# Residual adds as identity matmuls into PSUM, and second-LayerNorm sums from ScalarE, in an attention + GEGLU block

## The chip, the cores and the metric

One core of one Trainium2 chip runs the whole block in one launch. The metric is device time in microseconds (us). Before the change the median of the first four runs was 1486.33 us (1484.91 to 1489.46). The profile is one execution; its span is about 1.7 us shorter than the timed run.

Engine names in profile lines: PE is TensorE (matmul), PEld its weight load, DVE is VectorE, ACT is ScalarE, POOL is GpSimd.

## The reference

2048 tokens of width 512, 32 heads of width 16, FFN width 1792, all bf16:

```python
h  = x + attention(layernorm(x)) @ wo
h2 = h + (gelu(layernorm(h) @ w_gate) * (layernorm(h) @ w_up)) @ w_down
```

Two residual adds and a second LayerNorm (LN2) lie between the matmuls. They are what the change moves.

## The kernel before

The kernel is one list of "ticks", 1024 of them for the row maxima (phase 1) and 1024 for the exps (phase 2), 42 ticks apart. In each tick TensorE makes two score tiles that VectorE max-reduces and, of an earlier unit, two transposed score tiles that ScalarE exponentiates into bf16. A *unit* is 32 ticks: four heads against 512 queries. Eight units make a *chunk* of 512 tokens. Three PSUM banks serve phase 1 and three serve phase 2, and all four matmuls of a tick wait together:

```python
P.group_begin("pe")
t1  = p1_pair(tick // 32, tick % 32, gp1, signal_last=not p2_ok) if p1_ok else []
t2l = p2_pair(t2 // 32, t2 % 32, 1 - gp1) if p2_ok else []
P.group_end("pe")            # moves all waits of the four matmuls to the first
...                          # p1_consume: two max-reduces on VectorE
...                          # p2_consume: two exps on ScalarE
```

Everything else (Q/K/V projections, output projection, FFN) is cut into pieces of two or three matmuls, and one piece goes into each tick. When a piece is done, its PSUM bank has to be emptied; most items do so with an "evacuation" on ScalarE. Two kinds of item used VectorE instead. `item_oproj` (attention output projection, four per chunk) and `item_down` (FFN down projection, four per chunk):

```python
def item_oproj(b, c, qt):
    ...                                     # four matmuls into pbank[:, b, :]
    dve_late_ns[0] += 1480                  # asks for filler matmuls, see below
    P.op("dve", tensor_tensor(out=hh[:, qt, :], in0=pbank[:, b, :], in1=xres[:, xi, :], op=add))
    P.op("dve", bn_stats(out=stats2[:, t, :], in_=hh[:, qt, :]))
    P.op("dve", bn_aggr(out=mv2[:, t, :], in_=stats2[:, t, :]))
    ...                                     # POOL: rstd, -mean*rstd, normalise into hn_sb

def item_down(b, c, qt):
    ...                                     # fourteen matmuls into pbank[:, b, :]
    dve_late_ns[0] += 690
    P.op("dve", tensor_tensor(out=out_sb[:, oi, :], in0=pbank[:, b, :], in1=hh[:, qt, :], op=add))
    ...                                     # DMA to the output
```

(The lines are shortened: argument lists of the planner are left out.) After a tick with such VectorE work the loop adds filler matmuls, one for each 230 ns of it:

```python
if dve_late_ns[0] and p2_started and p1_ok:
    dummy(3 + p2_ring[0] % 3, dve_late_ns[0] // 230)
```

The fourth chunk's second half comes after all ticks; there is no attention to share time with any more. This is called the *tail*.

## Time and profile before

| what | before |
|---|---|
| median time | 1486.33 us (first four runs), 1489.15 (13 runs) |
| span of the profile | 1487.7 us |
| end of the last phase-1 unit | 1373.7 us |
| busy VectorE / ScalarE / TensorE | 89% / 86% / 77% |

The busy totals are the first part of the page:

```profile
PE 1142.3 (77%) x8558; PEld 310.6 (21%) x8558; DVE 1322.2 (89%) x2206; ACT 1274.8 (86%) x2414; POOL 453.1 (30%) x557
```

The groups of instructions (line, engine, operation, shapes, count; then busy time and mean ns of one; then idle time before them and what ended it):

```profile
L554 DVE TENSOR_REDUCE PM<-pbank 128x1 f32<-128x512 f32 x2048 | 1255.9, 683 | 62.3 <-PE pbank L595 49.3 <-PE pbank L545 12.0
L605 ACT ACTIVATE PT<-pbank 128x512 bf16<-128x512 f32 x2048 | 1116.6, 601 | 107.8 <-PE pbank L595 36.8
...
L695 DVE BATCH_NORM_STATS2 stats<-h_c 128x6 f32<-128x512 bf16 x16 | 11.1, 694 | 0.6
L794 DVE TENSOR_TENSOR out_sb<-pbank,h_c 128x512 bf16<-128x512 f32 x16 | 11.0, 686 | 56.9 <-PE pbank L787 56.9
L693 DVE TENSOR_TENSOR h_c<-pbank,xres 128x512 bf16<-128x512 f32 x16 | 10.9, 684 | 11.1 <-PE pbank L687 11.1
```

The first two groups are the attention itself. Busy time over count gives 0.613 us per max-reduce and 0.545 us per exp, so a tick of two of each needs 1.23 us on VectorE and 1.09 us on ScalarE. The mean duration (683 and 601 ns) is longer, because consecutive instructions of an engine overlap.

The timeline of VectorE around one oproj item shows the interruption. Columns: start, duration, engine, line, operation, shapes, count.

```profile
446.07 2.48 DVE L554 TENSOR_REDUCE PM<-pbank 128x1 f32<-128x512 f32 x4 [0.17 <-PE pbank L595]
448.47 0.68 DVE L693 TENSOR_TENSOR h_c<-pbank,xres 128x512 bf16<-128x512 f32 x1
449.19 0.69 DVE L695 BATCH_NORM_STATS2 stats<-h_c 128x6 f32<-128x512 bf16 x1
449.92 0.18 DVE L696 BATCH_NORM_AGGREGATE mv<-stats 128x2 f32<-128x6 f32 x1
450.01 2.45 DVE L554 TENSOR_REDUCE PM<-pbank 128x1 f32<-128x512 f32 x4
452.50 0.26 DVE L559 TENSOR_REDUCE NEGM<-PM 128x16 f32<-128x64 f32 x1
```

From 448.47 to 450.01 us the max-reduces stand still: 1.54 us. The last line (128x16) is the end of a unit. It comes once in 32 ticks, so the distance between two of these is the length of a unit, and that repeats to a few hundredths of a us. Here are the engines' busy times in five units, which differ in what else they hold: three ScalarE extras and nothing more; one oproj; three oproj; FFN (12 ScalarE extras); two down items.

```profile
core 0: us, PE busy (x) PEld busy (x) DVE busy (x) ACT busy (x) POOL busy (x), PEclk, DMA share, GB/s
372.02:411.37 39.35, 31.50 (x247) 7.48 (x246) 38.81 (x66) 35.88 (x68) 4.53 (x6) 1.00 0.01 1
411.37:452.50 41.13, 32.55 (x260) 8.41 (x258) 40.35 (x69) 36.27 (x69) 6.48 (x11) 1.00 0.05 14
452.50:497.21 44.71, 34.21 (x278) 9.96 (x275) 43.45 (x75) 37.67 (x72) 10.67 (x22) 1.00 0.00 1
538.37:579.87 41.50, 30.88 (x250) 7.75 (x246) 39.56 (x66) 39.42 (x77) 22.62 (x24) 1.00 0.00 1
704.34:745.00 40.66, 34.23 (x265) 8.96 (x262) 40.12 (x67) 36.07 (x69) 7.62 (x9) 1.00 0.02 8
```

The first unit is the attention alone, 39.35 us. One oproj makes it 41.13, three make it 44.71, two down items 40.66 (0.65 us per add). In the row with three oproj VectorE is busy 43.45 of 44.71 us and ScalarE only 37.67: VectorE sets these units. In the FFN row both are busy about 39.5 of 41.5.

In the tail the VectorE adds follow the matmuls at a steady distance:

```profile
1437.28 0.69 DVE L693 TENSOR_TENSOR h_c<-pbank,xres 128x512 bf16<-128x512 f32 x1 [1.37 <-PE pbank L687]
...
1440.28 0.69 DVE L693 TENSOR_TENSOR h_c<-pbank,xres 128x512 bf16<-128x512 f32 x1 [1.36 <-PE pbank L687]
...
1481.78 0.69 DVE L794 TENSOR_TENSOR out_sb<-pbank,h_c 128x512 bf16<-128x512 f32 x1 [2.33 <-PE pbank L787]
1484.81 0.69 DVE L794 TENSOR_TENSOR out_sb<-pbank,h_c 128x512 bf16<-128x512 f32 x1 [2.33 <-PE pbank L787]
```

That is 3.00 us between oproj items, 3.03 between down items; TensorE's matmuls make up most of it.

### The profile page before, as it was taken

What the parts mean: (1) busy time and instruction counts of PE and PEld (TensorE: products, weight loads), DVE (VectorE), ACT (ScalarE), POOL (GpSimd) and SP (SyncE); (2) the same over time, 40 slices, a digit from 0 to 9 for tenths busy, and PEclk for the clock granted to TensorE, in tenths of its full rate; (3) what the DMA queues carried; (4) which work ended last, traced back from release to release, by engine and by line L of the source; (5) the groups of instructions that cost most, each with busy time, mean ns of one, the idle gap of its engine ahead of it and who ended that gap; (6) DMA issues with size and microseconds to landing.
All of it is one profiled execution on the core that took longest, in us unless ns stands there. A gap on an engine that the chain in (4) does not pass through costs nothing.

```text
span 1487.7 us, 24868 instructions
## 1 busy us (share of the span) xinstructions
PE 1142.3 (77%) x8558; PEld 310.6 (21%) x8558; DVE 1322.2 (89%) x2206; ACT 1274.8 (86%) x2414; POOL 453.1 (30%) x557
## 2 busy tenths in 40 slices
PE   4977777777777777777887777777887777777879
PEld 2311111111112211111222211111222211111224
DVE  5989999998999999999999999999999999998023
ACT  3469999997998999999888999999888999999942
POOL 6001011110112255554112255554112255554130
PEclk9999999999999999999999999999999999999969
DMA  3000000012000000000000000000000000000000
GB/s 113 1 1 2 1 2 2 2 73 77 1 16 1 2 1 1 1 1 2 8 23 1 2 1 1 1 1 1 9 23 2 1 2 1 1 1 2 8 22 15
DMA packets 11531, 15.88 MB, mean 11 GB/s; under 512 B 1040, under 2 KB 9872, under 8 KB 11408
## 3 DMA queue, kind: packets, MB, share of 16 engines
q1 hardware_dynamic: 11408, 14.29, 2.8%
q8 instruction: 71, 1.16, 0.3%
q14 instruction: 52, 0.43, 0.1%
HBM read 11.80 MB, written 2.10 MB: 9 GB/s over the span
## 4 chain that ended last, share of the span: by engine, by line
DVE 37%; ACT 27%; PE 18%; issue 16%; POOL 1%; DMA 1%; SPq 0%; POOLq 0%; ACTq 0%
DVE PM L554 34%; ACT PT L605 23%; PE pbank L545 11%; PE pbank L787 2%; PE pbank L595 1%; PE pbank L480 1%; PE pbank L744 1%; PE pbank L763 1%; ACT OA L443 1%; ACT u_sb L443 1%; DVE stats L311 1%; DVE stats L695 1%; ACT g_sb L443 1%; DVE h_c L693 1%; PE pbank L687 1%
## 5 line engine op out<-in xcount | busy, mean ns | idle before, releaser
L554 DVE TENSOR_REDUCE PM<-pbank 128x1 f32<-128x512 f32 x2048 | 1255.9, 683 | 62.3 <-PE pbank L595 49.3
L605 ACT ACTIVATE PT<-pbank 128x512 bf16<-128x512 f32 x2048 | 1116.6, 601 | 107.8 <-PE pbank L595 36.8
L545 PE MATMUL pbank<-KT,QT 32*128 32x512 bf16 x2048 | 398.7, 384 | 301.4 <-DVE PM L554 169.2
L595 PE MATMUL pbank<-QT,KT 32*128 32x512 bf16 x2048 | 397.9, 385 | 3.2 <-ACT PT L605 2.7
L801 PE MATMUL pbank<-ones_bf,ident 128*128 128x512 bf16 x910 | 282.9, 384 | 1.3
L545 PEld LDWEIGHTS pbank<-KT,QT 32*128 32x128 bf16 x2048 | 103.8, 91 | 773.6 <-DVE PM L554 760.6
L639 POOL TENSOR_TENSOR LINV<-OAT,negone 128x16 f32<-128x16 f32 x32 | 93.3, 2916 | 351.6 <-ACT OAT L443 351.6
L616 PE MATMUL pbank<-PT,VA 128*17 128x512 bf16 x2048 | 156.7, 383 | 0.0
L565 POOL CAST ST<-NEGM 128x16 bf16<-128x16 f32 x32 | 8.1, 254 | 320.3 <-DVE NEGM L559 320.3
L595 PEld LDWEIGHTS pbank<-QT,KT 32*128 32x128 bf16 x2048 | 96.1, 91 | 22.4 <-ACT PT L605 21.9
L801 PEld LDWEIGHTS pbank<-ones_bf,ident 128*128 128x128 bf16 x910 | 61.7, 97 | 120.8 <-ACT PT L605 91.6
L722 POOL TENSOR_TENSOR w_sb<-g_sb 128x512 f32<-128x512 f32 x42 | 43.7, 1041 | 136.0 <-ACT g_sb L443 136.0
L744 PE MATMUL pbank<-hnT_c,wg_sb 128*128 128x512 bf16 x224 | 67.0, 392 | 0.9 <-ACT hnT_c L443 0.7
L763 PE MATMUL pbank<-hnT_c,wu_sb 128*128 128x512 bf16 x224 | 66.3, 388 | 0.0
L794 DVE TENSOR_TENSOR out_sb<-pbank,h_c 128x512 bf16<-128x512 f32 x16 | 11.0, 686 | 56.9 <-PE pbank L787 56.9
L787 PE MATMUL pbank<-wd_sb,GUT 128*128 128x512 bf16 x224 | 58.6, 382 | 2.2
L776 POOL TENSOR_TENSOR GUT<-th_sb,u_sb 128x512 bf16<-128x512 f32 x42 | 53.2, 1266 | 14.5 <-ACT u_sb L443 13.3
L724 POOL TENSOR_TENSOR w_sb<-w_sb,g_sb 128x512 f32<-128x512 f32 x42 | 53.3, 1269 | 3.5
L728 POOL TENSOR_TENSOR th_sb<-th_sb,g_sb 128x512 f32<-128x512 f32 x42 | 53.2, 1267 | 3.5
L616 PEld LDWEIGHTS pbank<-PT,VA 128*17 128x17 bf16 x2048 | 28.3, 87 | 58.7 <-issue 58.4
L441 ACT ACTIVATE KT<-pbank,kbias 128x512 bf16<-128x512 f32 x32 | 22.1, 689 | 19.2 <-PE pbank L480 19.2
L480 PE MATMUL pbank<-xnT,wk_pad 128*128 128x512 bf16 x128 | 37.8, 412 | 0.8
(75 smaller groups left out, 667.5 us busy)
## 6 DMA issues: line engine op xcount, KB each, us to landing
x_sb<-in_A_x_dram SPq DMA_DIRECT2D x4, 512.0 KB, 5.5
QT<-STG SPq DMA_DIRECT2D x128, 3.0 KB
xres<-in_A_x_dram SPq DMA_DIRECT2D x16, 128.0 KB, 2.2
out_dram<-out_sb SPq DMA_DIRECT2D x16, 128.0 KB, 1.7
wg_sb<-in_B_w_gate_dram SPq DMA_DIRECT2D x1, 1792.0 KB, 7.1
wu_sb<-in_B_w_up_dram SPq DMA_DIRECT2D x1, 1792.0 KB, 11.1
wd_sb<-in_B_w_down_dram SPq DMA_DIRECT2D x1, 1792.0 KB, 17.1
wqkv_sb<-in_A_wqkv_dram SPq DMA_DIRECT2D x1, 1536.0 KB, 10.3
```

The source lines that it names most:

```text
L545: P.op("pe", lambda e, g=g, b=b: e.matmul(pbank[:, b, :], QT[32 * g:32 * g + 32, c, slot, 128 * qt:128 * qt + 128], KT[32 * g:32 * g + 32, ...
L554: P.op("dve", lambda e, b=b, qt=qt, kc=kc, g=g: e.tensor_reduce(out=PM[:, par, qt, kc, g:g + 1], in_=pbank[:, b, :], axis=AX.X, op=ALU.max ...
L595: P.op("pe", lambda e, g=g, b=b: e.matmul(pbank[:, b, :], KT[32 * g:32 * g + 32, slot, 128 * kt:128 * kt + 128], QT[32 * g:32 * g + 32, c, ...
L605: P.op("act", lambda e, b=b, pi=pi: e.activation(out=PT[:, pi, :], in_=pbank[:, b, :], func=ACT.Exp), reads=[("pb", b)], writes=[("PT", pi)])
L616: P.op("pe", lambda e, g=g, kt=kt, pi=pi, slot=slot: e.matmul(pbank[32 * g:32 * g + 17, PVB, :], VA[:, kt, 4 * slot + g, :], PT[:, pi, :], ...
L639: P.op("pool", lambda e: e.tensor_tensor(out=li, in0=oat4[:, :, :, 16], in1=negone[:].rearrange("p (q g) -> p q g", g=4), op=ALU.pow), rea ...
L724: P.op(eng, lambda e: e.tensor_tensor(out=ws, in0=ws, in1=gs, op=ALU.mult), reads=[("w", par), ("g", par)], writes=[("w", par)])
L728: P.op(eng, lambda e: e.tensor_tensor(out=ts_, in0=ts_, in1=gs, op=ALU.mult), reads=[("th", par), ("g", par)], writes=[("th", par)])
L744: P.op("pe", lambda e, dc=dc: e.matmul(pbank[:, b, :], wg_sb[:, dc, 128 * fc:128 * fc + 128], hT[:, dc, :], start=(dc == 0), stop=(dc == 3 ...
L763: P.op("pe", lambda e, dc=dc: e.matmul(pbank[:, b, :], wu_sb[:, dc, 128 * fc:128 * fc + 128], hT[:, dc, :], start=(dc == 0), stop=(dc == 3 ...
L787: P.op("pe", lambda e, fc=fc: e.matmul(pbank[:, b, :], GUT[:, fc, 128 * qt:128 * qt + 128], wd_sb[:, fc, :], start=(fc == 0), stop=(fc == ...
L801: P.op("pe", lambda e: e.matmul(pbank[:, b, :], ident[:], ones_bf[:, 0:512], start=True, stop=True), reads=["ident", "ones_bf"], writes=[( ...
```

## The change

The intent is to relieve VectorE. The residual is added by TensorE: a matmul of the identity with the residual tile accumulates it into the same PSUM bank. ScalarE then copies the finished sum out, and its accumulator output gives the row sum of h. A second ScalarE pass (Square with accumulation) gives the sum of squares, and POOL makes mean and variance from the two sums. The tail keeps VectorE, with a copy in place of the add. The filler requests of these two items are dropped.

```diff
 def item_oproj(b, c, qt):
-    four matmuls, the last with stop=True
-    dve_late_ns[0] += 1480
-    dve: h = pbank + xres ; bn_stats(h) ; bn_aggr
-    return 2
+    four matmuls, none with stop
+    P.op("pe", matmul(pbank[:, b, :], ident[:], xres[:, xi, :], start=False, stop=True))
+    if tail_mode[0]:
+        dve: h = copy(pbank) ; bn_stats(h) ; bn_aggr ; ln2_tail ; return 3
+    P.op("act", activation(out=hh[:, qt, :], in_=pbank[:, b, :], func=Copy, accum_out=hsum[:, t:t+1]))
+    def sq():                     # put off while this or the last tick has a ScalarE extra
+        P.op("act", activation(out=sqj[:], in_=hh[:, qt, :], func=Square, accum_out=hsq[:, t:t+1]))
+        defer(1, lambda: ln2_from_sums(c, qt, t))     # POOL: mean, E[h^2] - mean^2, rstd, normalise
+    defer(2, sq)
+    return 3
 ...
 def item_down(b, c, qt):
-    fourteen matmuls, the last with stop=True
-    dve_late_ns[0] += 690
-    dve: out_sb = pbank + h
+    fourteen matmuls, none with stop
+    P.op("pe", matmul(pbank[:, b, :], ident[:], hh[:, qt, :], start=False, stop=True))
+    dve (tail): out_sb = copy(pbank)    else act: out_sb = Copy(pbank)
```

(Abbreviated; helpers and clean-ups without effect are left out.)

More of the change, by code (lines that the diff above doesn't have):

```diff
@@ L278, in bass_sequential_preLN__mha_block__geglu_ffn__prompt_kernel @@
         nmr1 = at("nmr1", [128, NT], FP32)
+        hsum = at("hsum", [128, NT], FP32)
+        hsq = at("hsq", [128, NT], FP32)
+        htmp = at("htmp", [128, NT], FP32)
+        sqj = at("sqj", [128, 512], BF16)
         pbank = es.enter_context(nc.psum_tensor("pbank", [128, 8, 512], FP32))
@@ L413, in defer @@
             deferred.append((dense.now + k, fn))
+        force = [False]
         def run_deferred(now, flush=False):
+            if flush:
+                force[0] = True
             i = 0
@@ L420, in run_deferred, with evac_act @@
                     i += 1
-        def halves(ap):
-            n = ap.shape[-1]
-            h = n // 2
-            idx0 = tuple([slice(None)] * (len(ap.shape) - 1) + [slice(0, h)])
-            idx1 = tuple([slice(None)] * (len(ap.shape) - 1) + [slice(h, n)])
-            return ap[idx0], ap[idx1]
         act_extra = set()
-        def evac_act(o_ap, i_ap, reads, writes, scale=None, extra=(), bias=None, split=False, then=None):
+        def evac_act(o_ap, i_ap, reads, writes, scale=None, extra=(), bias=None, then=None):
             act_extra.add(dense.now)
-            def one(o, i):
-                kw = {}
-                if scale is not None:
-                    kw["scale"] = scale
-                if bias is not None:
-                    P.op("act", lambda e: e.activation(out=o, in_=i, func=ACT.Identity, bias=bias, **kw), reads=list(reads) + ["kbias"], writes=writes, extra_deps=extra)
-                else:
-                    P.op("act", lambda e: e.activation(out=o, in_=i, func=ACT.Copy, **kw), reads=reads, writes=writes, extra_deps=extra)
-            if not split or not dense.single:
-                one(o_ap, i_ap)
-                if then is not None:
-                    then()
-                return
-            o0, o1 = halves(o_ap)
-            i0, i1 = halves(i_ap)
-            one(o0, i0)
-            for w in writes:
-                P.held.add(w)
-            def second():
-                for w in writes:
-                    P.held.discard(w)
-                one(o1, i1)
-                if then is not None:
-                    then()
-            defer(1, second)
+            kw = {}
+            if scale is not None:
+                kw["scale"] = scale
+            if bias is not None:
+                P.op("act", lambda e: e.activation(out=o_ap, in_=i_ap, func=ACT.Identity, bias=bias, **kw), reads=list(reads) + ["kbias"], writes=writes, extra_deps=extra)
+            else:
+                P.op("act", lambda e: e.activation(out=o_ap, in_=i_ap, func=ACT.Copy, **kw), reads=reads, writes=writes, extra_deps=extra)
+            if then is not None:
+                then()
         region = {}
@@ L498, in item_projV @@
                     yield 2
-            pv3 = pbank[:, b, :].rearrange("p (h i) -> p h i", i=16)
-            if False:
-                P.op("act", lambda e: e.activation(out=VA[:, t, 0:16, 0:16], in_=pv3[:, 0:16, :], func=ACT.Copy), reads=[("pb", b)], writes=[("V", t)])
-                P.held.add(("V", t))
-                def vsecond():
-                    P.held.discard(("V", t))
-                    P.op("act", lambda e: e.activation(out=VA[:, t, 16:32, 0:16], in_=pv3[:, 16:32, :], func=ACT.Copy), reads=[("pb", b)], writes=[("V", t)])
-                defer(1, vsecond)
-            else:
-                P.op("act", lambda e: e.activation(out=VA[:, t, :, 0:16], in_=pv3, func=ACT.Copy), reads=[("pb", b)], writes=[("V", t)])
+            evac_act(VA[:, t, :, 0:16], pbank[:, b, :].rearrange("p (h i) -> p h i", i=16), [("pb", b)], [("V", t)])
             qkv_left[0] -= 1
@@ L646, in item_ofin @@
             return 1
+        out_n = [0]
         chunk_units_done = {}
@@ L685, in item_oproj @@
             xi = qt
+            hh = h_c[c]
             for hc in range(4):
-                P.op("pe", lambda e, hc=hc: e.matmul(pbank[:, b, :], OnT[:, qt, hc, :], wo_sb[:, hc, :], start=(hc == 0), stop=(hc == 3)),
-                     reads=[("OH", qt), "wo"], writes=[("pb", b)], sig=(hc == 3))
+                P.op("pe", lambda e, hc=hc: e.matmul(pbank[:, b, :], OnT[:, qt, hc, :], wo_sb[:, hc, :], start=(hc == 0), stop=False),
+                     reads=[("OH", qt), "wo"], writes=[("pb", b)], sig=False)
@@ L689, in item_oproj @@
                 if hc == 1:
                     yield 2
-            hh = h_c[c]
-            dve_late_ns[0] += 1480
-            P.op("dve", lambda e: e.tensor_tensor(out=hh[:, qt, :], in0=pbank[:, b, :], in1=xres[:, xi, :], op=ALU.add),
-                 reads=[("pb", b), ("xres", xi)], writes=[("h", c, qt)], extra_deps=dQ)
-            P.op("dve", lambda e: e.bn_stats(out=stats2[:, t, :], in_=hh[:, qt, :]), reads=[("h", c, qt)], writes=[("stats2", t)])
-            P.op("dve", lambda e: e.bn_aggr(out=mv2[:, t, :], in_=stats2[:, t, :]), reads=[("stats2", t)], writes=[("mv2", t)])
@@ L697, in item_oproj @@
-            P.op("pool", lambda e: e.tensor_scalar(out=rstd2[:, t:t + 1], in0=mv2[:, t, 1:2], scalar1=EPS, scalar2=None, op0=ALU.add), reads=[("mv2", t)], writes=[("rstd2", t)])
-            P.op("pool", lambda e: e.tensor_tensor(out=rstd2[:, t:t + 1], in0=rstd2[:, t:t + 1], in1=nhalf[:, 0:1], op=ALU.pow), reads=[("rstd2", t), "nhalf"], writes=[("rstd2", t)])
-            P.op("pool", lambda e: e.tensor_tensor(out=nmr2[:, t:t + 1], in0=mv2[:, t, 0:1], in1=rstd2[:, t:t + 1], op=ALU.mult), reads=[("mv2", t), ("rstd2", t)], writes=[("nmr2", t)])
@@ L700, in item_oproj @@
-            P.op("pool", lambda e: e.tensor_scalar(out=nmr2[:, t:t + 1], in0=nmr2[:, t:t + 1], scalar1=-1.0, scalar2=None, op0=ALU.mult), reads=[("nmr2", t)], writes=[("nmr2", t)])
-            P.op("pool", lambda e: e.tensor_scalar(out=hn_sb[:, qt, :], in0=hh[:, qt, :], scalar1=rstd2[:, t:t + 1], scalar2=nmr2[:, t:t + 1], op0=ALU.mult, op1=ALU.add),
+            P.op("pe", lambda e: e.matmul(pbank[:, b, :], ident[:], xres[:, xi, :], start=False, stop=True),
+                 reads=["ident", ("xres", xi)], writes=[("pb", b)], sig=True)
@@ new lines, in item_oproj @@
+            if tail_mode[0]:
+                P.op("dve", lambda e: e.tensor_copy(out=hh[:, qt, :], in_=pbank[:, b, :]), reads=[("pb", b)], writes=[("h", c, qt)], extra_deps=dQ)
+                P.op("dve", lambda e: e.bn_stats(out=stats2[:, t, :], in_=hh[:, qt, :]), reads=[("h", c, qt)], writes=[("stats2", t)])
+                P.op("dve", lambda e: e.bn_aggr(out=mv2[:, t, :], in_=stats2[:, t, :]), reads=[("stats2", t)], writes=[("mv2", t)])
+                ln2_tail(c, qt, t)
+                return 3
@@ new lines, in item_oproj @@
+            act_extra.add(dense.now)
+            P.op("act", lambda e: e.activation(out=hh[:, qt, :], in_=pbank[:, b, :], func=ACT.Copy, accum_out=hsum[:, t:t + 1]),
+                 reads=[("pb", b)], writes=[("h", c, qt), ("hsum", t)], extra_deps=dQ)
+            def sq():
+                if not force[0] and ((dense.now in act_extra) or ((dense.now - 1) in act_extra and dense.now - 1 != sq_t0[0])):
+                    defer(1, sq)
+                    return
+                act_extra.add(dense.now)
+                P.op("act", lambda e: e.activation(out=sqj[:], in_=hh[:, qt, :], func=ACT.Square, accum_out=hsq[:, t:t + 1]),
+                     reads=[("h", c, qt)], writes=[("sqjunk",), ("hsq", t)])
+                defer(1, lambda: ln2_from_sums(c, qt, t))
@@ new lines, in item_oproj, with ln2_from_sums @@
+            sq_t0 = [dense.now]
+            defer(2, sq)
+            return 3
+        def ln2_from_sums(c, qt, t):
+            hh = h_c[c]
+            tt_ = slice(t, t + 1)
+            P.op("pool", lambda e: e.tensor_scalar(out=mv2[:, t, 0:1], in0=hsum[:, tt_], scalar1=1.0 / D, scalar2=None, op0=ALU.mult), reads=[("hsum", t)], writes=[("mv2", t)])
+            P.op("pool", lambda e: e.tensor_tensor(out=htmp[:, tt_], in0=mv2[:, t, 0:1], in1=mv2[:, t, 0:1], op=ALU.mult), reads=[("mv2", t)], writes=[("htmp", t)])
+            P.op("pool", lambda e: e.tensor_scalar(out=rstd2[:, tt_], in0=hsq[:, tt_], scalar1=1.0 / D, scalar2=EPS, op0=ALU.mult, op1=ALU.add), reads=[("hsq", t)], writes=[("rstd2", t)])
+            P.op("pool", lambda e: e.tensor_tensor(out=rstd2[:, tt_], in0=rstd2[:, tt_], in1=htmp[:, tt_], op=ALU.subtract), reads=[("rstd2", t), ("htmp", t)], writes=[("rstd2", t)])
+            ln2_finish(c, qt, t)
@@ new lines, in ln2_tail, with ln2_finish @@
+        def ln2_tail(c, qt, t):
+            tt_ = slice(t, t + 1)
+            P.op("pool", lambda e: e.tensor_scalar(out=rstd2[:, tt_], in0=mv2[:, t, 1:2], scalar1=EPS, scalar2=None, op0=ALU.add), reads=[("mv2", t)], writes=[("rstd2", t)])
+            ln2_finish(c, qt, t)
+        def ln2_finish(c, qt, t):
+            hh = h_c[c]
+            tt_ = slice(t, t + 1)
+            P.op("pool", lambda e: e.tensor_tensor(out=rstd2[:, tt_], in0=rstd2[:, tt_], in1=nhalf[:, 0:1], op=ALU.pow), reads=[("rstd2", t), "nhalf"], writes=[("rstd2", t)])
+            P.op("pool", lambda e: e.tensor_tensor(out=nmr2[:, tt_], in0=mv2[:, t, 0:1], in1=rstd2[:, tt_], op=ALU.mult), reads=[("mv2", t), ("rstd2", t)], writes=[("nmr2", t)])
+            P.op("pool", lambda e: e.tensor_scalar(out=nmr2[:, tt_], in0=nmr2[:, tt_], scalar1=-1.0, scalar2=None, op0=ALU.mult), reads=[("nmr2", t)], writes=[("nmr2", t)])
+            P.op("pool", lambda e: e.tensor_scalar(out=hn_sb[:, qt, :], in0=hh[:, qt, :], scalar1=rstd2[:, tt_], scalar2=nmr2[:, tt_], op0=ALU.mult, op1=ALU.add),
@@ L729, in later @@
             def later():
-                if dense.single and (dense.now in act_extra or (dense.now - 1) in act_extra):
+                if not force[0] and (dense.now in act_extra or (dense.now - 1) in act_extra):
                     defer(1, later)
@@ L778, in item_up @@
             return 2
-        out_n = [0]
         def item_down(b, c, qt):
@@ L785, in item_down @@
                 yield ("wait", 7)
+            hh = h_c[c]
             for fc in range(NFC):
-                P.op("pe", lambda e, fc=fc: e.matmul(pbank[:, b, :], GUT[:, fc, 128 * qt:128 * qt + 128], wd_sb[:, fc, :], start=(fc == 0), stop=(fc == NFC - 1)),
-                     reads=[("GUT", fc), "wd"], writes=[("pb", b)], sig=(fc == NFC - 1))
+                P.op("pe", lambda e, fc=fc: e.matmul(pbank[:, b, :], GUT[:, fc, 128 * qt:128 * qt + 128], wd_sb[:, fc, :], start=(fc == 0), stop=False),
+                     reads=[("GUT", fc), "wd"], writes=[("pb", b)], sig=False)
                 if fc % 3 == 2:
                     yield 3
+            P.op("pe", lambda e: e.matmul(pbank[:, b, :], ident[:], hh[:, qt, :], start=False, stop=True),
+                 reads=["ident", ("h", c, qt)], writes=[("pb", b)], sig=True)
             oi = out_n[0] % 2; out_n[0] += 1
-            hh = h_c[c]
-            dve_late_ns[0] += 690
-            P.op("dve", lambda e: e.tensor_tensor(out=out_sb[:, oi, :], in0=pbank[:, b, :], in1=hh[:, qt, :], op=ALU.add),
-                 reads=[("pb", b), ("h", c, qt)], writes=[("osb", oi)], extra_deps=dG)
+            if tail_mode[0]:
+                P.op("dve", lambda e: e.tensor_copy(out=out_sb[:, oi, :], in_=pbank[:, b, :]), reads=[("pb", b)], writes=[("osb", oi)], extra_deps=dG)
+            else:
+                evac_act(out_sb[:, oi, :], pbank[:, b, :], [("pb", b)], [("osb", oi)], extra=dG)
             P.dma("sp", lambda e: e.dma_start(out=outv[:, t, :], in_=out_sb[:, oi, :]), ("out", oi), reads=[("osb", oi)], writes=[("outd", t)])
-            return 2
+            return 3
         def dummy(b, n):
```

## The prediction

> **What bounds the kernel now.** Span 1487.7 us; the page's busy table gives VectorE 89%, ScalarE 86%, TensorE 77%. The main part (1024 ticks, to 1374 us) issues per tick two score tiles that VectorE max-reduces and two that ScalarE exponentiates; a tick lasts as long as the slower. Busy time over count: a max-reduce occupies VectorE 0.613 us (1255.9/2048), an exp ScalarE 0.545 (1116.6/2048): 1.23 against 1.09 us per tick.
>
> The timeline shows one row-max finish (128x16 reduce) per unit of 32 ticks; unit lengths price the extras:
> - 3 ScalarE extras, no VectorE extra: 39.35 us. An isolated evacuation costs one 0.17 us VectorE gap.
> - 12 ScalarE extras (FFN): 41.5, so about 0.23 us each of their 0.6.
> - one oproj item: add 0.68, stats 0.69, aggregate 0.18, in all 1.54 us. Unit with one: 41.13; with three: 44.71.
> - two down adds: 40.66, +0.65 each.
>
> After 1374 us VectorE idles and ScalarE runs exps back to back (39 in 21.68 us): every extra there costs its full 0.55. From 1424 us a serial tail follows.
>
> **What the change moves** (from the built instruction order). VectorE loses 12 add+stats+aggregate groups and 8 exposed down adds. ScalarE gains 12 copies with accumulated sum, 12 squares, 11 output evacuations (3 of them after 1374 us). TensorE gains 32 identity matmuls, loses 96 fillers (910 to 814). No third table load.
>
> **Costed, on the critical path.**
> - Removed: 12 x 1.54 + 8 x 0.65 = 23.7 us, all critical.
> - Added in the main part: 8 isolated output copies x 0.2 = 1.6; and 24 copies and squares of h. In the units with three oproj the extras rise from 8 to 14, some in adjacent ticks, so ScalarE becomes the limit: (64 + 14) x 0.545 = 42.5 us plus bubbles, against 44.71. They gain about 2 us each, not 4.6. With the units of one oproj (-1.1, twice -1.7) and of two downs (twice -0.85): about -11 us.
> - After 1374 us: 3 copies x 0.55 = +1.6.
> - Tail (VectorE keeps its part, copy for add): the Trainium skill, "VectorE: DVE Perf Modes", section "Why PSUM operands drop a tier", says an fp32 PSUM operand caps VectorE at 1x, so the copy should cost about the add's 0.69 us; this trace has no such copy. The identity matmul joins the chain: oproj matmuls there start 0.43 us apart (low clock), down matmuls 0.216 (14 in 3.02 us): 4 x 0.43 + 5 x 0.216 = +2.8.
> - Accumulator output: the skill's "ScalarE: Activation LUTs", "What it computes", lists it as part of ACTIVATE; no instruction of this trace shows its price. I allow 0 to 0.1 us each.
>
> Sum: -11 + 1.6 + 2.8 + about 1 = -6 to -9. The main part's identity matmuls fit where fillers were.
>
> **Predicted:** 1478.5 us, 1472 to 1484. Faster by over 2%: 0.01; within 2%: 0.98; slower: 0.01.
>
> **What would show it.** Unit lengths: three oproj about 42.7, one oproj about 40, two downs about 39.8, FFN unchanged at 41.5. VectorE busy down about 30 us, ScalarE up 19 to 22. In oproj units waits move from the max-reduce to the exp. Tail about 3 us longer: oproj spacing 3.0 to 3.4, down spacing 3.02 to 3.24.
>
> **What would make it wrong.** A costly accumulator read (0.2 us or more) eats the gain; squares hidden as well as FFN extras make it 12 us; a late normalisation stalling TensorE.

## The result, and the profile after

The changed kernel is correct. Its median is 1479.21 us (1478.92 to 1481.50, 9 runs) beside 1489.15 us for the kernel before (13 runs in all). The ratio is 0.994, 95% interval 0.9930 to 0.9949. A ratio here is the mean time of one kernel's fast runs over that of the other's of the same rounds, so not quite the ratio of the medians. A clear gain of 0.6%.

The busy totals:

```profile
PE 1128.3 (76%) x8494; PEld 304.9 (21%) x8494; DVE 1301.4 (88%) x2159; ACT 1290.3 (87%) x2473; POOL 459.4 (31%) x593
```

VectorE lost 20.8 us of busy time, ScalarE gained 15.5. The groups that are new:

```profile
L682 ACT ACTIVATE sqj<-h_c 128x512 bf16<-128x512 bf16 x12 | 7.6, 632 | 0.0
...
L675 ACT ACTIVATE h_c<-pbank 128x512 bf16<-128x512 f32 x12 | 7.3, 607 | 0.0
...
L802 DVE CAST out_sb<-pbank 128x512 bf16<-128x512 f32 x5 | 3.5, 692 | 61.2 <-PE pbank L798 61.2
...
L675 ACT ACTIVATION_READ_ACCUMULATOR h_c<-pbank 128x1 f32 x12 | 2.6, 218 | 0.0
L682 ACT ACTIVATION_READ_ACCUMULATOR sqj<-h_c 128x1 f32 x12 | 2.4, 203 | 0.0
```

Each accumulator output shows as an instruction of its own, ACTIVATION_READ_ACCUMULATOR, 0.20 to 0.22 us long. What it takes in the stream is less. ScalarE's timeline inside the first unit with three oproj items:

```profile
461.39 0.60 ACT L675 ACTIVATE h_c<-pbank 128x512 bf16<-128x512 f32 x1
461.87 0.21 ACT L675 ACTIVATION_READ_ACCUMULATOR h_c<-pbank 128x1 f32 x1
461.96 2.28 ACT L578 ACTIVATE PT<-pbank 128x512 bf16<-128x512 f32 x4
464.13 0.60 ACT L440 ACTIVATE OnT<-pbank 128x512 bf16<-128x512 bf16 x1
464.60 1.11 ACT L578 ACTIVATE PT<-pbank 128x512 bf16<-128x512 f32 x2
...
468.25 0.63 ACT L682 ACTIVATE sqj<-h_c 128x512 bf16<-128x512 bf16 x1
468.77 0.20 ACT L682 ACTIVATION_READ_ACCUMULATOR sqj<-h_c 128x1 f32 x1
468.86 1.08 ACT L578 ACTIVATE PT<-pbank 128x512 bf16<-128x512 f32 x2
```

A copy of h takes 0.48 us until the read starts, and the next exp starts 0.09 us after that (461.87 to 461.96, 468.77 to 468.86). An evacuation takes 0.47 us (464.13 to 464.60), the square 0.52.

The five units again, in the same order as before:

```profile
core 0: us, PE busy (x) PEld busy (x) DVE busy (x) ACT busy (x) POOL busy (x), PEclk, DMA share, GB/s
370.75:410.11 39.36, 31.52 (x247) 7.49 (x246) 38.81 (x66) 35.89 (x68) 4.53 (x6) 1.00 0.01 1
410.11:450.07 39.96, 31.51 (x255) 7.95 (x253) 39.02 (x66) 36.84 (x71) 4.53 (x6) 1.00 0.05 15
450.07:492.76 42.69, 31.46 (x263) 8.72 (x260) 39.82 (x65) 40.92 (x86) 14.73 (x38) 1.00 0.00 1
533.93:575.42 41.49, 30.87 (x250) 7.74 (x246) 39.55 (x66) 39.41 (x77) 22.60 (x24) 1.00 0.01 1
699.89:739.87 39.98, 33.41 (x261) 8.63 (x258) 39.16 (x65) 36.84 (x71) 7.61 (x9) 1.00 0.02 8
```

The three-oproj unit is now 42.69 us. VectorE is busy 39.82 of it, ScalarE 40.92: the leader has changed. ScalarE executes 86 instructions there: 64 exps, 15 extras and 7 accumulator reads, against 72 before. The unit without these items and the FFN unit are unchanged to 0.01 us.

The waits of TensorE for the phase-1 tiles in the three-oproj unit (who waited for whom, us in total, times, longest), first before, then after:

```profile
PEld pbank L545 <- DVE PM L554: 24.0, 31, 1.3
...
PE pbank L545 <- DVE PM L554: 7.3, 22, 0.8
...
PE pbank L545 <- ACT PT L605: 3.1, 7, 0.5
```

```profile
PEld pbank L518 <- DVE PM L527: 25.1, 32, 1.0
...
PE pbank L518 <- ACT PT L578: 6.7, 14, 0.6
PE pbank L518 <- DVE PM L527: 4.3, 16, 0.6
```

The matmuls' waiting for VectorE fell and their waiting for ScalarE rose. The weight loads (PEld) wait for VectorE as much as before, so this view alone does not tell which engine sets the unit; e7 below does.

The tail:

```profile
1426.96 0.69 DVE L669 CAST h_c<-pbank 128x512 bf16<-128x512 f32 x1 [1.80 <-PE pbank L666]
...
1430.39 0.69 DVE L669 CAST h_c<-pbank 128x512 bf16<-128x512 f32 x1 [1.79 <-PE pbank L666]
...
1471.16 0.69 DVE L802 CAST out_sb<-pbank 128x512 bf16<-128x512 f32 x1 [2.54 <-PE pbank L798]
1474.40 0.69 DVE L802 CAST out_sb<-pbank 128x512 bf16<-128x512 f32 x1 [2.55 <-PE pbank L798]
```

The oproj distance is 3.43 us instead of 3.00, the down distance 3.24 instead of 3.03. The copy from PSUM takes the same 0.69 us as the add did.

Where the 10.4 us of span went, from the unit ends of the two profiles:

| part | before | after | change |
|---|---|---|---|
| three units with three oproj | 44.71, 44.71, 44.70 | 42.69, 42.68, 42.69 | -6.1 |
| one unit with one oproj | 41.13 | 39.96 | -1.2 |
| two units with two downs and one oproj | 42.18, 42.17 | 40.61, 40.60 | -3.1 |
| two units with two downs | 40.66, 40.66 | 39.98, 39.99 | -1.4 |
| the other 24 units | | | -1.2, of it -1.1 in the first unit (start-up) |
| from the last unit's end to the end | 114.0 | 116.6 | +2.6 |

The eight changed units give 11.7 us. The start-up differs from run to run for any kernel here (the first unit ended between 74.9 and 76.3 us in these profiles, and the second was mostly either 46.2 or 47.5 us long), so it is not counted.

### The profile page after: what moved, and what is told of

Read it like the earlier page. It is cut to its first block, busy times and chain, and to the rows that moved or that the text cites. A ratio compares the mean times of both kernels' runs of the same rounds, so it can differ in the third digit from the quotient of the medians.

```text
span 1477.3 us, 24742 instructions
## 1 busy us (share of the span) xinstructions
PE 1128.3 (76%) x8494; PEld 304.9 (21%) x8494; DVE 1301.4 (88%) x2159; ACT 1290.3 (87%) x2473; POOL 459.4 (31%) x593
## 4 chain that ended last, share of the span: by engine, by line
ACT 32%; DVE 31%; PE 19%; issue 16%; POOL 1%; DMA 1%; SPq 0%; POOLq 0%; ACTq 0%
DVE PM L527 30%; ACT PT L578 26%; PE pbank L518 12%; PE pbank L794 2%; PE pbank L568 1%; PE pbank L462 1%; PE pbank L751 1%; ACT OA L440 1%; PE pbank L770 1%; ACT u_sb L440 1%; DVE stats L315 1%; ACT g_sb L440 1%; PE pbank L662 1%; ACT sqj L682 0%; ACT OnT L440 0%
## 5 line engine op out<-in xcount | busy, mean ns | idle before, releaser
L810 PE MATMUL pbank<-ones_bf,ident 128*128 128x512 bf16 x814 | 258.4, 384 | 1.2
L810 PEld LDWEIGHTS pbank<-ones_bf,ident 128*128 128x128 bf16 x814 | 52.3, 97 | 110.4 <-ACT PT L578 96.2
L802 DVE CAST out_sb<-pbank 128x512 bf16<-128x512 f32 x5 | 3.5, 692 | 61.2 <-PE pbank L798 61.2
L462 PE MATMUL pbank<-xnT,wq_pad 128*128 128x512 bf16 x128 | 38.0, 384 | 0.1
```

What stands on the lines that cost most here:

```text
L810: P.op("pe", lambda e: e.matmul(pbank[:, b, :], ident[:], ones_bf[:, 0:512], start=True, stop=True), reads=["ident", "ones_bf"], writes=[( ...
```

## The experiments

Theory S, as the expectations call it: the gain is VectorE's removed work, given back in part because ScalarE becomes the one that sets the three-oproj units, and again at the end, where VectorE was idle and the identity matmul lies on the chain. Rivals: the accumulator reads eat the gain (A); TensorE's longer matmul groups do (B); part of the gain came from dropping the fillers (C); or it lies in the down items alone.

Unit lengths in us by kind, from each run's profile (with three oproj: first of its kind where they agree within 0.03):

| kernel | median us | 3 oproj | 1 oproj | 2 down | last unit's end to the end |
|---|---|---|---|---|---|
| before | 1489.15 | 44.71 | 41.13 | 40.66 | 114.0 |
| changed | 1479.21 | 42.69 | 39.96 | 39.98 | 116.6 |
| changed, again (e11) | 1479.37 | 42.68 | 39.96 | 39.99 | 117.2 |
| e1, oproj only | 1482.23 | 42.68 | 39.96 | 40.65 | 115.1 |
| e2, down only | 1487.93 | 44.71 | 41.13 | 39.99 | 114.8 |
| e3, no accumulators | 1476.53 (1 run) | 42.05 | 39.88 | 39.98 | 115.0 |
| e4, no identity matmuls | 1478.84 (1 run) | 42.68 | 39.96 | 39.98 | 114.2 |
| e5, before without fillers | 1492.51 | 45.68, 45.49, 46.72 | 41.13 | 40.65 | 113.4 |
| e7, no squares | 1477.07 (1 run) | 41.18 | 39.96 | 39.99 | 116.5 |
| e6, late adds on VectorE | 1478.19 | 42.66 | 39.96 | 39.98 | 114.1 |
| e12, e6 again | 1477.09 | 42.68 | 39.97 | 39.98 | 113.7 |
| e10, squares on POOL | 1478.72 | 42.89, 43.09, 42.31 | 39.95 | 39.98 | 113.6 |
| e13, three of four squares on POOL | 1473.70 | 41.52 | 39.96 | 39.98 | 113.2 |

All listed times are fast runs, or single runs (marked). One run of the kernel before, beside e1 to e4, took 3062.98 us and does not count as fast.

### e1 and e2: each half alone

```diff
 e1: changed kernel, item_down of the kernel before
 e2: kernel before, item_down of the changed kernel
```

> The changed kernel with the down items put back to the VectorE add (oproj items stay changed). Theory S (ScalarE, not the removed VectorE work, sets a unit with several oproj items): unit with three oproj items 42.7 us as in the changed kernel, unit with one 39.96, unit with two down items back to 40.66, unit with two downs and one oproj 41.2 to 41.3. The four units of the oproj part keep about 9 us of the 11.7 us gain of the main part. From the last row-max finish to the first tail evacuation 47.9 us as before (no output copies on ScalarE). Time about 7 us under before. Rival (the gain comes mostly from the down items): under 3 us.

> The kernel before with only the down items changed. Theory S: unit with two downs 40.0 us, two downs and one oproj 41.5, three oproj unchanged 44.7; the main part gains about 2.7 us and the end gives back about 1.2 us of output copies on ScalarE and 0.9 us of identity matmuls: time 0 to 1 us under before. Rival: 5 us or more under before.

e1: 1482.23 us, ratio 0.9957 (0.9935 to 0.9978). Units as expected: 42.68, 39.96, 40.65, and 41.01 with two downs and one oproj (a little better than expected). e2: 1487.93 us, ratio 0.9993 (0.9977 to 1.0008). The halves add up unit by unit: e1 shortens the eight units by 9.6 us, e2 by 2.1, together 11.7, which is what the whole change does. So there is no interaction in the main part, and the oproj half carries four fifths of it. The units of e2 with two downs and one oproj took 41.77 us, not the 41.5 expected. The down half alone is not clear of noise overall. In its profile 0.8 of the 2.1 us are lost again at the end (114.8 against 114.0): output copies on ScalarE compete with exps (49.1 instead of 47.9 us to the first tail evacuation), and identity matmuls join the chain (down distance 3.24 us).

### e3: what the accumulator outputs cost

```diff
-activation(out=hh[:, qt, :], in_=pbank[:, b, :], func=Copy, accum_out=hsum[:, t:t+1])
+activation(out=hh[:, qt, :], in_=pbank[:, b, :], func=Copy)
-activation(out=sqj[:], in_=hh[:, qt, :], func=Square, accum_out=hsq[:, t:t+1])
+activation(out=sqj[:], in_=hh[:, qt, :], func=Square)
```

> Wrong result on purpose: the changed kernel without the accumulated sums (constants in their place); copies and squares stay. Theory S with a cheap read (next exp starts 0.09 us after the read begins): 6 reads fewer in a three-oproj unit, 0.5 us less, about 42.2; one-oproj unit 39.9. Rival A (the accumulator read costs its shown 0.21 us and drains the engine): 41.4 or less.

Its output is wrong, which doesn't matter for the time. The three-oproj unit fell from 42.69 to 42.05 us. It holds seven reads (one square of the neighbouring item falls into it), so 0.09 us each, just the start-to-start distance of the timeline. Rival A, 0.21 us for each, would have shown 1.5 us. The reads are real but small.

### e4: what the identity matmuls cost

```diff
-P.op("pe", matmul(pbank[:, b, :], ident[:], xres[:, xi, :], start=False, stop=True))
-P.op("pe", matmul(pbank[:, b, :], ident[:], hh[:, qt, :], start=False, stop=True))
+                            # the last projection matmul has stop=True again
```

> Wrong result on purpose: the changed kernel without any identity matmul. Theory S: all main units within 0.1 us of the changed kernel (42.7, 39.96, 39.98), as TensorE is not the limit; oproj spacing in the tail back to 3.0 us from 3.43, down spacing back to 3.02 from 3.24; what the end gains overall tells whether the earlier clock rise was due to them. Rival B (the longer matmul groups delay the exps): three-oproj unit 0.6 us shorter or more.

Its output is wrong, which doesn't matter for the time. None of the eight changed units moved by more than 0.02 us: TensorE takes the extra matmul for free there, and rival B is out. In the tail the distances went back to 3.00 and 3.02 us, and the stretch after the last unit got 2.4 us shorter (116.6 to 114.2; 117.2 in e11, so one profile each gives 2.4 to 3.0). The time of the run shows little of it, because the last unit ended 2.2 us later in this profile, most of it (1.8 us) from the first two units.

### e7: ScalarE relieved of the squares

```diff
-P.op("act", activation(out=sqj[:], in_=hh[:, qt, :], func=Square, accum_out=hsq[:, t:t+1]))
+                            # hsq holds a constant
```

> Wrong result on purpose: the changed kernel without the squares (and their reads). Theory S (ScalarE sets the three-oproj unit): from 14 extras to 11, so near the 41.17 us of the unit that has 11 extras today, plus up to 0.3 for the three reads left: 41.2 to 41.5, from 42.69. One-oproj unit 39.7 from 39.96. Rival B (TensorE or the item order sets it): stays at 42.0 or more.

The three-oproj unit fell to 41.18 us, four squares and their reads fewer, 0.38 us each. Busy times of that unit in e7 (columns as in the tables of units above):

```profile
452.72:493.90 41.18, 31.27 (x263) 8.57 (x260) 39.40 (x65) 39.06 (x78) 14.69 (x38) 1.00 0.00 1
```

ScalarE's busy time fell by 1.9 us and the unit by 1.5, with the same number of instructions on VectorE: so ScalarE set the unit in the changed kernel. (Three squares fewer were expected, four are missing, so 41.18 us lies just under the expected range.) That taking still more work from VectorE would not help there follows from this, but was not run. The one-oproj unit did not move (39.7 was expected): its item's square falls into the next unit.

### e5: the fillers

```diff
-dve_late_ns[0] += 1480
-dve_late_ns[0] += 690
```

(in the kernel before)

> The kernel before without the filler matmuls that follow its oproj and down items (96 fewer). Theory S: they end before VectorE is free again, so unit lengths stay (41.13, 44.71, 40.66) and the time is within 2 us of before. Rival C (part of the change's gain came from dropping fillers): three-oproj unit 0.5 us shorter or more.

This expectation failed. e5 is slower than before: ratio 1.0028 (1.0012 to 1.0044), and the three-oproj units rose from 44.71 to between 45.5 and 46.7 us. The first of them, and 4 us of it after its first oproj item (last three columns: granted clock, DMA share, GB/s):

```profile
452.54:498.22 45.68, 34.42 (x262) 8.61 (x261) 43.93 (x75) 37.56 (x73) 11.32 (x23) 0.89 0.00 1
...
468.00:472.00 4.00, 3.94 (x24) 0.68 (x24) 3.65 (x6) 3.89 (x9) 0.62 (x1) 0.65 0.00 0
```

The granted clock is 0.89 there, where it is 1.00 in the same unit of before. Within the unit, 4 us stretches after an oproj item go down to 0.65 and 0.57. Read in half-microsecond windows, such a stretch is 0.50 for about 3.4 us (467.4 to 470.8) and 1.00 on both sides. The Trainium skill, "TensorE: Matmul & The Clock Gate", section "What's actually happening", describes a gate that sets the clock by how busy TensorE has been, with a half-rate state and windows of about 3.4 us. The two rates and the length agree: clocks of 0.50 and 1.00 over longer stretches are also what the tail and the main part show here. What differs is the trigger: the page has the clock fall after an idle window of about 3.4 us, while here TensorE waited 1.72 us for VectorE's oproj work, and the measurement decides. In e5 there are 12 such waits, one for each oproj item before the tail; nine are followed by a half-rate stretch, three are not. In the kernel before there is no half-rate stretch anywhere between 350 and 1420 us: there the fillers kept the clock up. What a drop costs varies (three of them lengthened one unit by 1.0 us and another by 2.0, and one unit with a single drop not at all). So rival C has the wrong sign: dropping the fillers did not make the change faster. The change loses nothing by it, as the stall that they covered is gone as well: the longest wait of its phase-1 matmuls in the three-oproj unit is 0.6 us, and the clock there is 1.00. Whether fillers would still gain something there was not tested.

### e6 and e12: late adds back on VectorE

```diff
+last = fc == NFC - 1 and (tail_mode[0] or dense.now >= 32 * NU)   # phase 1 is over
 P.op("pe", matmul(..., start=(fc == 0), stop=last))
-P.op("pe", matmul(pbank[:, b, :], ident[:], hh[:, qt, :], start=False, stop=True))
+if not last: P.op("pe", matmul(pbank[:, b, :], ident[:], hh[:, qt, :], start=False, stop=True))
+if last: dve: out_sb = pbank + h        # as in the kernel before; item_oproj in the tail likewise
```

> The changed kernel, but with the plain VectorE adds (no identity matmul) wherever the row-max phase is over and VectorE is idle: three down items after 1361 us and the whole tail. Main units as in the changed kernel (42.69, 39.98). From last row-max finish to the first tail evacuation 47.9 us instead of 49.1; oproj spacing 3.0, down spacing 3.02. Expected 1 to 3 us under the changed kernel, the spread being the moment at which the clock rises in the tail. If the identity matmuls paid for themselves by keeping the clock up: equal.

> e6_late_adds_dve once more beside the changed kernel: 1 to 2.5 us under it; its end (last row-max finish to the end) 2 to 2.5 us shorter in the profile.

e6: 1478.19 us, ratio to before 0.9924 (0.9912 to 0.9936). e12 ran beside the changed kernel (e11) on one chip:

> The changed kernel once more, on the same chip, as the yardstick for the two others: 1478.5 to 1481.5 us, ratio 0.993 to 0.995.

e11: 1479.37 us, ratio 0.9936 (0.9923 to 0.9950); e12: 1477.09 us, ratio 0.9920 (0.9907 to 0.9932). The end is 113.7 us against 117.2 in these two profiles. From the last unit's end to the first tail evacuation it is 47.9 us instead of 49.1, so the three output copies cost 1.2 us there; the rest is the tail. That is 3.5 us, more than the 2 to 2.5 expected; against the first profile of the changed kernel (116.6) it is 2.9. The intervals of the two ratios overlap, but the units of the main part are equal and the gain lies just where the edit is.

### e8: each engine's own waits

```diff
-P.group_begin("pe")
 t1  = p1_pair(..., signal_last=True)
 t2l = p2_pair(...)
-P.group_end("pe")
```

> As e6_late_adds_dve, but each tick's two row-max tiles wait for VectorE alone and signal on their own, where now all four tiles of a tick wait for both engines together. If the price of ScalarE extras (0.22 us each where ScalarE has slack) comes from this coupling: units with 3 extras 39.0 from 39.35, with 9 extras 40.2 from 40.67, FFN 41.0 to 41.5, in all 5 to 10 us less. If it comes from ScalarE's own load, FFN stays at 41.5 and only the isolated 0.17 us gaps go. If the four tiles lose their overlap in TensorE: slower than e6.

A failure: 1549.90 us, ratio 1.0410 (1.0396 to 1.0424). Units that were 40.67 us became 41.24 (FFN 41.49 became 41.40), TensorE's busy share rose to 94%, and three units after 325 us took 62 to 66 us. In them:

```profile
400.00:450.00 50.00, 48.71 (x188) 8.25 (x187) 32.28 (x51) 28.11 (x53) 3.52 (x2) 0.50 0.00 1
```

TensorE is busy 48.71 of 50 us at a clock of 0.50. The four tiles of a tick start together in the changed kernel (300.19 and 300.20 us, for example); here they often start in two pairs (300.78 and 300.98, 301.94 and 302.23 us). That this lost overlap takes TensorE to its limit is the likely reading; why the clock stayed down for those three units was not tested. (The kernel before also drops to 0.50, from 342 to 348 us, after a 6.2 us wait of TensorE for a DMA, but there the clock comes back.) Whether the joint wait is what makes an FFN unit 41.5 us long, with both engines busy 95%, therefore stays open.

### e10 and e13: the squares on POOL

ScalarE sets the three-oproj units and POOL is 31% busy, so the squares can move there. POOL multiplies h by itself (128x512, 1.04 us) and adds halves nine times; in e10's first such item this takes 4.5 us in all (450.32 to 454.82), a little more than the 3 to 4 expected. This is a correct kernel on top of e6:

```diff
-P.op("act", activation(out=sqj[:], in_=hh[:, qt, :], func=Square, accum_out=hsq[:, t:t+1]))
+P.op("pool", tensor_tensor(out=sqj[:], in0=hh[:, qt, :], in1=hh[:, qt, :], op=mult))
+n = 256
+while n > 1:
+    P.op("pool", tensor_tensor(out=sqj[:, 0:n], in0=sqj[:, 0:n], in1=sqj[:, n:2*n], op=add)); n //= 2
+P.op("pool", tensor_tensor(out=hsq[:, t:t+1], in0=sqj[:, 0:1], in1=sqj[:, 1:2], op=add))
```

> Correct version of the run without squares, on top of e6_late_adds_dve: the square and its sum run on POOL (one multiply, nine halving adds, an estimate of 3 to 4 us per item from POOL's 1.04 us multiply and 0.2 us small operations here), which is 30% busy. Theory S (the square's place on ScalarE costs the three-oproj units 1.5 us each): these units 41.2 us from 42.69, all others as before, the end as in e6: 4 to 5 us under e6_late_adds_dve, about 1473.5 to 1474.5 us. If POOL's longer chain delays the normalisation: TensorE waits on POOL in these units and they stay above 41.5.

e10: 1478.72 us, three-oproj units 42.89, 43.09 and 42.31: nothing gained, so this expectation failed too. In the first of them TensorE has a wait that the changed kernel does not have:

```profile
PEld pbank L548 <- POOL ST L541: 2.0, 1, 2.0
...
PE pbank L548 <- POOL ST L541: 1.7, 1, 1.7
```

The chain of the chunk's first item kept POOL busy from 450.3 to 457.9 us, just when the row-max values of a finished unit (their VectorE line is at 452.6) needed four small POOL instructions before TensorE could transpose them. TensorE stood still for 1.7 us and its clock was 0.56 to 0.59 from 460 to 464 us. The second such unit shows the same wait and a clock of 0.64 for 4 us, the third the same wait (1.6 us) and no loss of clock in the stretches after it; it is the shortest of the three. e13 puts that one square back on ScalarE and leaves the other three on POOL:

```diff
-defer(1, sq)
+if qt == 0: defer(2, sq_act)       # ScalarE, as in the changed kernel
+else:       defer(1, sq)           # POOL
```

> As e10_square_pool, but the first square of each chunk goes back to ScalarE, because POOL's chain for it (450.3 to 457.9 us) held up the four POOL casts of the row-max, TensorE then waited 1.7 us and its clock fell to 0.56 for 4 us. If that was the whole loss: no wait of the row-max transpose on POOL, granted clock 1.00 in these units, the three-oproj units 41.5 to 41.7 us (three squares fewer at the 0.38 us measured) against 42.69, all others unchanged, 3 to 4 us under e6_late_adds_dve: 1473.5 to 1475.5 us. If POOL's work delays TensorE elsewhere too: 42.3 or more.

e13: correct, 1473.70 us (1473.56 to 1474.94), ratio to before 0.9903 (0.9886 to 0.9919). The wait is gone, and the three-oproj units are 41.52, 41.53 and 41.53 us:

```profile
451.77:493.29 41.52, 31.34 (x263) 8.61 (x260) 39.55 (x65) 39.41 (x80) 24.91 (x66) 1.00 0.00 1
```

VectorE and ScalarE are level now (39.55 and 39.41 us busy). This version beats both kernels: its interval lies wholly below that of the changed kernel (0.9930 to 0.9949).

## Why the prediction was right

The predicted time was 1478.5 us with a range of 1472 to 1484; measured 1479.21. That the two lie within 0.7 us is partly luck. Measured from 1486.33 us, the median of the first four runs, 1478.5 takes off 7.8 us; the 13 runs of the kernel before have a median of 1489.15, and the gain against that is 9.9 us (0.6%, about 9 us, by the ratio). So the gain was forecast somewhat too small, and a starting value 2.8 us too low made up for it. Nor do two of the sums close: the units listed for the main part add up to -12.2, not -11, and -11 + 1.6 + 2.8 + 1 is -5.6, just outside the -6 to -9 that it is said to be. In the profiles the three terms came out as -11.7, +1.2 and +1.4, together -9.1 (the other 1.2 of the 10.4 us of span are start-up and small change); the "about 1" has no counterpart. Point by point:

- *VectorE's removed work is all critical, 23.7 us.* Right in kind: the one-oproj unit was 1.78 us longer than the plain one, with 1.54 us of VectorE work and one ScalarE extra more; the two-down units 1.31 us, twice 0.65; and all units without such work stayed as they were.
- *ScalarE becomes the limit in the three-oproj units, 42.5 us plus bubbles; these units gain about 2 us each, not 4.6.* Right: 42.69, a gain of 2.02, and e7 shows that ScalarE sets them. The sum behind it was right by luck. It used 14 extras of 0.545 us and no reads. The trace has 15 extras of about 0.48 us and 7 reads of 0.09 us; with exps 0.54 us apart (after the last row-max 14 in a row last 7.85 us and 16 last 8.93, so two more take 1.08) an estimate is 64 x 0.54 + 15 x 0.48 + 7 x 0.09 = 42.4 us. One extra too few, each priced 0.07 us too high.
- *One oproj about 40, two downs about 39.8, FFN unchanged.* 39.96, 39.98, and 41.5 as before. The two-down units gained 0.7 us each, not 0.85: an isolated copy on ScalarE costs about 0.3 us instead of 0.2 (39.98 less 39.36, over two).
- *About -11 us in the main part.* -11.7.
- *After 1374 us +1.6.* Measured +1.2: the time to the first tail evacuation went from 47.9 to 49.1 us.
- *Tail +2.8.* Distances exactly as said (3.43 and 3.24 us), but the tail as a whole took only 1.4 us more in this profile, as its clock rose earlier: the second FFN product came 1.73 us after the first, where before it took 2.67. In the second profile of the same kernel (e11) it came after 1.90, and the end was 0.6 us longer; so the moment of the rise is not a constant of the kernel. The end differs by 0.4 to 0.7 us between two profiles of the same code (e6 and e12, changed and e11). By e4 the identity matmuls account for about 2.4 us. So the mechanism was right, and the size of this term, +2.8 for what came out as +1.4 to +2.1, was the largest miss of the sum.
- *The copy from PSUM costs what the add costs.* 692 ns against 684 and 686. The Trainium skill, "VectorE: DVE Perf Modes", section "Why PSUM operands drop a tier", was the ground for it, and the trace agrees that the copy is no faster than the add.
- *Accumulator output 0 to 0.1 us.* 0.09 us. The Trainium skill, "ScalarE: Activation LUTs", section "What it computes", lists the output but not that it comes as a second instruction.
- *VectorE busy down about 30 us, ScalarE up 19 to 22.* Wrong in size: 20.8 and 15.5. I added durations, and the page's busy time counts overlapping instructions once. That explains only a part: the groups of the two kernels differ by 26.1 us on VectorE (35.9 before, 9.8 after, as the four groups of these items are listed), not by 30, and the max-reduces' own busy time rose by 2.1.
- *The identity matmuls fit where fillers were.* They fit (e4), but what the fillers had done for the kernel before was not in the prediction at all; e5 showed it, against the expectation for it.

## What to carry to other kernels

When two engines run level in a loop, price a move of work by the unit it lands in: there VectorE's work was worth its full time only until ScalarE took the lead, and of 23.7 us removed 11.7 arrived. Move work only in the stage where the source is the limit: the same edit after the last row-max, where VectorE was idle, cost 2.6 us in one profile and 3.2 in another, and taking it back there was free gain. A mostly idle third engine is worth using, even if it is slower, provided its long job does not sit in front of a short one that TensorE waits for; and a matmul that looks useless may be what holds the clock (e5).

## What the Trainium skill lacked or had wrong

- "ScalarE: Activation LUTs", "What it computes": it names the accumulator output but not its price. Here it shows as a separate instruction ACTIVATION_READ_ACCUMULATOR of 0.20 to 0.22 us, which takes 0.09 us of the engine's stream (e3: seven reads fewer, 0.64 us less).
- "GPSIMD Engine Reference", opening: it calls the engine the wrong choice for ordinary elementwise arithmetic. Its ground is that VectorE is faster; where VectorE and ScalarE are both full, that is too strong here: three squares and their sums moved to POOL, about 4.5 us each but hidden, made the three-oproj units 1.16 us shorter than with ScalarE's faster square (e13 against the changed kernel).
- "TensorE: Matmul & The Clock Gate", "What's actually happening": the two rates agree with the clock that e5 and e10 lost (0.89 over a unit, 0.56 over 2 us), but the page has the half rate come after an idle window of about 3.4 us, and here waits of 1.72 us (e5, nine of twelve) and 1.7 us (e10, two of three) were followed by it. No page gives the price of a short stall in a loop limited by other engines: in e10 a wait of 1.6 to 1.7 us left these units 0.8 to 1.6 us longer than in e13 (42.31 to 43.09 against 41.5), the longer ones with the lost clock, although e10 has one square less on ScalarE.
